# A fused recurrence and long-convolution kernel whose order of work is a table: the table is replaced

## The chip, the core and the metric

The kernel runs on one core of one Trainium2 chip. A core has a matrix engine (TensorE, PE in the profile; its weight loads are shown apart as PEld), a vector engine (VectorE, DVE), a scalar engine (ScalarE, ACT), a general engine (GpSimd, POOL) and SyncE (SP), which here only issues DMA transfers. Matrix results go to PSUM, which has 8 banks; everything else is in SBUF or in device memory. The metric is the device time of one execution in microseconds (us), smaller is better. The kernel before has a median of 460.08 us of three runs, 459.45 to 461.24.

## What is computed

Two layers, one behind the other, on four batches of 6272 steps with 256 channels. The first is a gated linear recurrence, the second a gated long convolution done by Fourier transform:

```python
def _attn_ref(x, f_logit, lower_bound):
    sig = 1.0 / (1.0 + np.exp(-f_logit))
    f = lower_bound + (1.0 - lower_bound) * sig
    for t in range(S):
        h = f[:, t] * h + (1.0 - f[:, t]) * x[:, t]
        y[:, t] = h
def _moe_ref(x, w_proj, filter_fft, w_out):
    x1, x2, x3 = split(x @ w_proj)
    x2_conv = np.fft.irfft(np.fft.rfft(x2, axis=1) * np.fft.rfft(filter_fft, axis=0), axis=1)
    return (x1 * x2_conv * x3) @ w_out
```

## The kernel before

**An order that is data.** The kernel first describes its work as 2410 operations (`op`), each with a kind, the engines that may run it and the tiles it reads and writes. Nothing is scheduled by that: `ORDER` is a string of three-character words, and each word names an operation, an engine and, for TensorE's work, the PSUM bank. `emit` runs through the table and issues the operations one after the other; each engine thus gets its own queue in the order of the table, and works it strictly in that order.

```python
            word = a * 4096 + b * 64 + c
            yield word // 64, self.ENGINES[word // 8 % 8], word % 8
```

**The head.** The filter of 6272 x 256 is loaded in 13 parts (`ff`, L622), rounded where needed (`fr`), rotated by matmuls (`rot`, L637), moved out of PSUM (`f2`), transformed in two steps (`FF1` at L661 with evacuations `afs`, `FF2` at L679 with `hw`), and the spectrum H is stored to device memory (`hst`, L688). Matmuls on a unit matrix (`warm`, L603, two in each operation) compute nothing that is used; the table says where they stand.

**The recurrence** (`hgrn`). Each batch has 13 chunks of 512 steps (the last of 128). A chunk is loaded (`load`, L334: the gate f and then x; three buffers each), goes through the sigmoid on ScalarE (`sig`, L337) and a product on GpSimd (`u`, L339), is turned by transposes on TensorE (`su`, L351, two halves of the channels), the gate is finished (`f`, on ScalarE L364 or VectorE L366), and VectorE scans it (`scan`, L372). The scans of one half of the channels follow each other, chunk by chunk. The beginning of h is copied behind its end (`wrap`, by GpSimd, ScalarE or a DMA issued by SP at L301), since the convolution is cyclic.

**The convolution** of a batch. `P` (L725) applies the part W2 of the projection, 12 groups, and needs all scans of its batch; the evacuations `x2` go to ScalarE (L291) or VectorE (L296). Then 16 units of 8 channel pairs go through a forward transform (`F1`, L737, evacuated by `A`; `F2`, L795), the product with the spectrum loaded from H (`H`, L772; the product directly out of PSUM by VectorE at L816, which the table calls MUL, or a copy and a product `pm` on GpSimd at L825), and the inverse transform (`I2`, L835, evacuated by `Th`). Small operations (`mini`, `zm`, `slot`) treat one special frequency.

**The gates** x1 and x3 (`x13`, L400) run beside it. x1 is always copied out of PSUM (`xs`); x3 is either multiplied with it right out of PSUM by VectorE (MUL, L422), or copied, with the product `z` left to GpSimd (L431).

**The output** (`phase_o`): 13 groups of the last inverse transform (`I1`, L869), the product `y` on VectorE (L875), the output projection (`proj`, L887), its evacuation `o` and the store (L911).

The batches overlap: the chunks of batch b+1 are scanned during the second half of batch b and its output, a stretch that is called a turnover below. A bank is taken again when its evacuation is done, and `SP` issues loads, stores, the reads of H and some of the `wrap` copies in one queue, in the table's order, each waiting there until its tile is free or ready.

## Time and profile before

| | us |
|---|---|
| median of the runs | 460.08 |
| span of the profiled execution | 458.7 |
| TensorE busy | 444.4 |
| VectorE busy | 406.4 |
| ScalarE busy | 400.5 |
| GpSimd busy | 301.9 |

The time of a run is a little above the span, which counts from the first to the last instruction. "Busy" is the time in which at least one instruction of the engine was running. The groups of a profile are given as line, engine, operation, out<-in, shapes and count, then busy time and the mean duration of one in ns, then the idle time of that engine just before them with what ended it. A chain of waits names, from the last instruction back, what each step waited for. Batch 0's `P` begins at 75.5 us, batch 1's at 171, batch 2's at 272.6 and batch 3's at 371.2.

### The profile page before, as it was taken

How to read it: one execution, taken by the hardware profiler on the slowest of the kernel's cores; microseconds unless marked ns; L12 is line 12 of the kernel's file. 1: busy time of each engine (PE TensorE's matmuls, PEld its weight loads, DVE VectorE, ACT ScalarE, POOL GpSimd, SP SyncE). 2: the span in 40 equal slices, each digit the busy share in tenths (PEclk: the TensorE clock that was granted, in tenths of full speed). 3: DMA queues.
4: the chain of work that ended last, by engine and by line, in shares of the span. 5: the costliest groups of instructions: out<-in, count | busy, mean ns of one | idle time of the engine just before them, and what ended most of it. 6: DMA issues, size and time to landing. Idle time of an engine off the chain costs nothing.

```text
span 458.7 us, 14602 instructions
## 1 busy us (share of the span) xinstructions
PE 444.4 (97%) x6009; PEld 346.8 (76%) x6009; DVE 406.4 (89%) x459; ACT 400.5 (87%) x551; POOL 301.9 (66%) x279
## 2 busy tenths in 40 slices
PE   8998999999999999999999999999999999999996
PEld 6777777867766889777668879767768798777785
DVE  8389998699999997999999986999999984999974
ACT  4899998999999988989998969999999869889563
POOL 5377993179899742988996525979896503878500
PEclk9999999999999999999999999999999999999999
DMA  8998999957898898368869897388789542576077
GB/s 321 384 374 300 339 402 372 334 149 210 253 334 273 287 302 325 122 195 298 289 236 317 311 309 298 139 300 282 232 318 307 188 186 93 184 227 201 34 285 292
DMA packets 45298, 121.53 MB, mean 265 GB/s; under 512 B 4400, under 2 KB 8496, under 8 KB 45232
## 3 DMA queue, kind: packets, MB, share of 16 engines
q1 hardware_dynamic: 45232, 120.60, 74.8%
q8 instruction: 47, 0.77, 0.7%
q14 instruction: 19, 0.16, 0.1%
HBM read 86.12 MB, written 31.98 MB: 257 GB/s over the span
## 4 chain that ended last, share of the span: by engine, by line
PE 64%; DVE 12%; ACT 8%; DMA 7%; issue 5%; POOL 2%; SPq 1%; DVEq 0%; ACTq 0%; POOLq 0%
PE PS L400 15%; PE PS L725 9%; PE PS L835 9%; PE PS L351 6%; PE PS L887 6%; PE PS L795 6%; PE PS L737 6%; DVE HA L372 5%; DMA X<-in_moe_filter_fft_dram 4%; DVE ys L875 3%; PE PS L661 3%; DMA XT<-in_x_dram 2%; PE PS L869 2%; ACT fTs L364 2%; DMA out_dram<-PP 2%
## 5 line engine op out<-in xcount | busy, mean ns | idle before, releaser
L339 POOL TENSOR_TENSOR XT<-XT,FL 128x1024 f32<-128x1024 f32 (+1 forms) x49 | 109.7, 2243 | 53.9 <-ACT FL L337 47.3
L372 DVE TENSOR_TENSOR_SCAN HA<-fTs,HA,PS 128x512 f16<-128x512 f32 (+1 forms) x96 | 113.2, 1204 | 1.8 <-ACT fTs L364 1.0
L400 PE MATMUL PS<-HA,W 128*128 128x490 f16 (+1 forms) x416 | 102.9, 368 | 1.7 <-issue 0.7
L825 POOL TENSOR_TENSOR PP<-HA,Hu 98x1008 f16<-98x1008 f16 x40 | 83.9, 2104 | 8.0 <-ACT HA L291 3.9
L291 ACT CAST HA<-PS 128x1024 f16<-128x1024 f32 (+1 forms) x98 | 79.1, 834 | 5.3 <-PE PS L737 2.7
L431 POOL TENSOR_TENSOR zt<-gx 128x490 f16<-128x490 f32 (+1 forms) x37 | 44.9, 1219 | 43.0 <-issue 15.6
L875 DVE TENSOR_TENSOR ys<-PS,zt 128x1024 fp32r<-128x1024 f32 (+1 forms) x52 | 58.7, 1152 | 10.0 <-PE PS L869 7.0
L816 DVE TENSOR_TENSOR PP<-PS,Hu 98x1008 f16<-98x1008 f32 x56 | 65.8, 1202 | 0.9 <-issue 0.5
L364 ACT ACTIVATE fTs<-PS,cc 128x512 f32<-128x512 f32 (+1 forms) x85 | 56.1, 675 | 5.8 <-PE PS L351 4.8
L887 PE MATMUL PS<-Wo,ys 128*128 128x256 f32 x392 | 58.1, 294 | 1.6 <-DVE ys L875 1.3
L400 PEld LDWEIGHTS <-W 128*128 128x128 f16 x416 | 34.8, 97 | 31.6 <-issue 8.1
L835 PEld LDWEIGHTS <-PP 98*128 98x128 f16 x1024 | 50.0, 97 | 10.8 <-issue 1.8
L835 PE MATMUL PS<-VV,PP 98*128 98x98 f16 x1024 | 55.9, 206 | 0.7 <-DVE PP L816 0.5
L887 PEld LDWEIGHTS PS<-Wo,ys 128*128 128x128 f32 x392 | 49.8, 189 | 6.4 <-DVE ys L875 1.4
L291 ACT CAST Th<-PS 128x784 f16<-128x784 f32 x59 | 48.3, 821 | 5.7 <-PE PS L835 5.2
L293 ACT ACTIVATE gx<-PS 128x490 f32<-128x490 f32 (+1 forms) x86 | 49.7, 585 | 2.4 <-PE PS L400 1.0
L337 ACT ACTIVATE FL<-FL 128x1024 f32<-128x1024 f32 (+1 forms) x49 | 49.2, 1009 | 0.0
L422 DVE TENSOR_TENSOR zt<-PS,gx 128x490 f16<-128x490 f32 (+1 forms) x67 | 42.8, 650 | 2.7 <-PE PS L400 1.2
L725 PE MATMUL PS<-W,HA 128*128 128x256 f16 x392 | 44.6, 273 | 0.2
L725 PEld LDWEIGHTS <-HA 128*128 128x128 f16 x392 | 43.0, 142 | 1.2 <-issue 0.2
L351 PE MATMUL PS<-iden,FL 64*128 64x64 f32 x736 | 41.9, 230 | 1.1 <-DVE Hx L296 0.5
L351 PEld LDWEIGHTS PS<-iden,FL 64*128 64x128 f32 x736 | 31.3, 138 | 14.3 <-DVE HA L372 2.6
(129 smaller groups left out, 738.6 us busy)
## 6 DMA issues: line engine op xcount, KB each, us to landing
FL<-in_f_logit_dram SPq DMA_DIRECT2D x45, 512.0 KB, 5.6
XT<-in_x_dram SPq DMA_DIRECT2D x45, 512.0 KB, 6.2
Hu<-H SPq DMA_DIRECT2D x39, 512.0 KB, 4.7
out_dram<-osb SPq DMA_DIRECT2D x22, 512.0 KB, 4.4
out_dram<-PP SPq DMA_DIRECT2D x16, 512.0 KB, 5.2
Hx<-H SPq DMA_DIRECT2D x13, 512.0 KB, 4.5
out_dram<-HA SPq DMA_DIRECT2D x10, 512.0 KB, 4.9
X<-in_moe_filter_fft_dram SPq DMA_DIRECT2D x9, 512.0 KB, 7.3
```

The costliest lines, as they stand in the source:

```text
L291: nc.scalar.copy(dst, src)
L339: op("u", {"POOL": 0.1 + 0.553 * nb}, lambda e, xt=xt, ft=ft: nc.gpsimd.tensor_tensor(xt, xt, ft, op=AOP.mult), r=[("ft", k)], w=[("xt", k)])
L351: nc.tensor.transpose(bank(pb)[:, at[p] + j:at[p] + hn:nb], src[ps, j, cols], iden[ps, ps])
L364: nc.scalar.activation(fT, sT, AF.Identity, scale=by, bias=1.0)
L372: nc.vector.tensor_tensor_scan(h, fT, bank(pb)[:, 512 - hn:512 + hn], init, op0=AOP.mult, op1=AOP.add),
L400: nc.tensor.matmul(PS[:, p, 0:n], W13[:, kh, js], HA[:, HB[kh] + t0:HB[kh] + t0 + n], start=(kh == 0), stop=(kh == 1))
L725: nc.tensor.matmul(pp[:, r - r0, :], column(HB[kh], q_of(r)), W2[:, kh, :], start=(kh == 0), stop=(kh == 1))
L816: nc.vector.tensor_tensor(pr, px.unsqueeze(1).broadcast_to([TB, 2, UE, 63]), hh, op=AOP.mult)
L825: nc.gpsimd.tensor_tensor(pr, spec[:, o, :, 1:64].unsqueeze(1).broadcast_to([TB, 2, UE, 63]), hh, op=AOP.mult)
L835: nc.tensor.matmul(PS[:, ib + o, pr * TB:(pr + 1) * TB], PP[:TB, k, o, n, 2 * pr:2 * pr + 2, :], v[:TB], start=(n == 0), stop=(n == 1))
L875: nc.vector.tensor_tensor(late["ys"][:, yk, :, 0:rn * 128], PS[:, cb:cb + 2, 0:rn * 128], late["zt"][:].rearrange("p k r m -> p k (r m)") ...
L887: nc.tensor.matmul(po[:, i, :], late["ys"][:, yk, kh, i * 128:(i + 1) * 128], Wo[:, kh, :], start=(kh == 0), stop=(kh == 1))
```

## The change

All operations, tiles and functions stay. Only the string `ORDER` is another one. Its first line, before and after:

```diff
 ORDER = (
-    "AAYA+gBFgAMYABIAgVACIBBgAvWBMgAeUBTgAxSAdVBIgAkWBPgA9YANIAmUAoWA/TBGRBADBCYBogBDTBWgAtVAPIBNVAOABagBEDADgBdgBHBBhg"
+    "AAYAlXABIAMYACIANIAhRAPIBTgAkSAiWAaVAfVAgXApQAdVAnSBBgA+gBIgBFgAwXAqSAuUAbSAcXAjXBMgBPgBagBdgBWgA9YBJYBUSAtXArQAeW"
...
 )
```

Decoded, the two tables differ as follows.

| operations | engines before | engines after |
|---|---|---|
| x2 (48) | ScalarE 30, VectorE 18 | ScalarE 24, VectorE 24 |
| xs (208) | ScalarE 117, VectorE 24, direct product 67 | ScalarE 106, VectorE 19, direct product 83 |
| spectrum product (128) | direct 83, copy on VectorE 2, on ScalarE 43 | direct 85, copy on VectorE 0, on ScalarE 43 |
| f2 (13) | ScalarE 11, VectorE 2 | ScalarE 8, VectorE 5 |
| f (104) | ScalarE 85, VectorE 19 | ScalarE 86, VectorE 18 |
| A (64) | ScalarE 55, VectorE 9 | ScalarE 56, VectorE 8 |
| Th (64) | ScalarE 59, VectorE 5 | ScalarE 61, VectorE 3 |
| wrap (48) | GpSimd 26, SP 19, ScalarE 3 | GpSimd 23, SP 25 |

Direct products by batch: 20, 16, 15, 16 before and 21, 22, 16, 24 after. 1285 operations keep their engine and get another PSUM bank. On TensorE 559 of the 770 operations stand in another place, by three places on average; on VectorE the operations that both tables give it move by at most four places. TensorE changes between kinds that use half of its rows (transposes, F2, I1, FF2) and kinds that use all of them 252 times before and 250 times after. The larger moves on the queues, in the order in which each engine works (* is a count):

```text
TensorE, head, before:  warm*8 rot*3 warm rot*3 warm*3 rot warm*2 rot*5 warm*2 rot warm*3 FF1*4 warm FF2 FF1 warm FF2 FF1 su ...
TensorE, head, after:   warm*16 rot warm*4 rot warm rot warm rot*3 warm rot*2 warm*2 rot*5 warm FF1*4 FF2 FF1*3 FF2 su*2 ...
TensorE, batch 0, before:  x13*7 P*12 x13*4 F1*2 ...   (around last)
TensorE, batch 0, after:   x13*5 P*5 x13 P x13 P x13 P*2 x13 P*3 x13*3 F1*2 ...
TensorE, tail, before:  I1 proj*2 warm*5 I1 proj
TensorE, tail, after:   I1 proj I1 proj*2 warm*4
SP, filter and first loads, before:  ff0 2 1 4 6 3 5 12 7 8, lower_bound, ff9 10 11, then loads
SP, filter and first loads, after:   ff6 1 0 3 2 4 5 8 9 7 10 11, lower_bound, ff12, then loads
SP, end of batch 2, before:  f11 x11 store f/x12 ...   (x12 ahead of f12)
SP, end of batch 2, after:   f11 store f12 x11 x12 store ...
```

The last two lines name the loads of the last two chunks of batch 3, f for the gate and x for the input.

More of the change, by code (lines that the diff above doesn't have):

```diff
@@ L193 @@
+    "kgRkdskYokhPkipkjYidNigYikYilSkkUkPYdFQklXkUYkZYkmMknvkoYimCkpSkeYkqKdGAk4UkuQkzWkvIkrSksCk0OkwQk9Sk1Wk5Mk6Uk2GkxI"
+    "k+KlCQlHWk/Sk7ElDIlEUlMQlACdHgktglFEk3gkygk8glBglGglIOlNIlRSlJWlKGlSKlOUlPElLglQglWQlXIlbSlTWlYUlgQlUGlcKlVglZElag"
+    "lhIldSllUliQleClfglmMlnSloKlpgA8XA5XA4XA6XljAlkg"
 )
```

123 lines of the change are left out of this document (60 added, 63 removed).

## The prediction

> **What bounds the kernel now.** I read first the page's busy line and the line on the chain that ended last, then one table of stretches with each engine's busy time, cut where the chain changes character.
>
> ```profile
> span 458.7 us, 14602 instructions
> PE 444.4 (97%) x6009; PEld 346.8 (76%) x6009; DVE 406.4 (89%) x459; ACT 400.5 (87%) x551; POOL 301.9 (66%) x279
> PE 64%; DVE 12%; ACT 8%; DMA 7%; issue 5%; POOL 2%; SPq 1%; DVEq 0%; ACTq 0%; POOLq 0%
> ```
> TensorE is idle for 458.7 - 444.4 = 14.3 us of the span and carries 64% of the chain. The profiled execution spans 458.7 us; the median of the runs is 460.08, so 1.4 us lies around the span, and I add it at the end.
>
> ```profile
> core 0: us, PE busy (x) PEld busy (x) DVE busy (x) ACT busy (x) POOL busy (x), PEclk, DMA share, GB/s
> 0.00:23.35 23.35, 20.99 (x111) 16.51 (x112) 13.73 (x44) 16.21 (x17) 10.78 (x29) 1.00 0.92 353
> 23.35:35.60 12.25, 12.15 (x132) 9.56 (x134) 10.42 (x12) 11.14 (x14) 9.59 (x12) 1.00 0.97 357
> 35.60:56.00 20.40, 18.62 (x266) 14.57 (x266) 19.67 (x22) 19.93 (x30) 17.08 (x14) 1.00 0.91 321
> 56.00:75.50 19.50, 19.45 (x228) 14.38 (x229) 19.20 (x23) 18.89 (x28) 15.93 (x23) 1.00 1.03 382
> 75.50:86.20 10.70, 10.70 (x100) 10.65 (x99) 5.73 (x6) 9.09 (x11) 0.00 (x0) 1.00 0.96 344
> 86.20:130.00 43.80, 43.09 (x637) 30.90 (x634) 41.56 (x46) 41.30 (x60) 34.35 (x30) 1.00 0.75 236
> 130.00:171.00 41.00, 39.18 (x639) 30.05 (x633) 40.40 (x42) 38.37 (x57) 31.82 (x24) 1.00 0.87 294
> 171.00:243.00 72.00, 71.89 (x966) 54.39 (x966) 67.09 (x71) 65.85 (x96) 56.98 (x46) 1.00 0.71 249
> 243.00:272.60 29.60, 28.49 (x488) 24.27 (x489) 28.92 (x29) 24.80 (x34) 15.32 (x11) 1.00 0.91 301
> 272.60:343.00 70.40, 70.00 (x948) 52.61 (x949) 64.36 (x70) 66.67 (x96) 57.21 (x47) 1.00 0.76 270
> 343.00:371.20 28.20, 26.83 (x474) 23.09 (x471) 27.11 (x27) 24.19 (x33) 14.30 (x9) 1.00 0.70 244
> 371.20:381.60 10.40, 10.40 (x96) 10.09 (x96) 5.69 (x5) 7.09 (x9) 0.00 (x0) 1.00 0.36 141
> 381.60:431.80 50.20, 50.18 (x645) 36.07 (x646) 45.11 (x55) 43.61 (x63) 38.52 (x37) 1.00 0.47 151
> 431.80:458.70 26.90, 22.45 (x314) 19.66 (x312) 17.40 (x17) 13.33 (x14) 0.00 (x0) 1.00 0.65 260
> ```
> Three kinds of stretch stand here. In the middle of each batch (171 to 243, 272.6 to 343, 381.6 to 431.8) TensorE is busy to within 0.4 us: it is the bound, and its work is the same in both tables. In the turnovers from one batch to the next (243 to 272.6, 343 to 371.2, the end of 130 to 171) VectorE is busy to within 1.1 us, with the scans of the next batch and the products y of this one, and TensorE loses 1.11, 1.37 and at most 1.82 us. The third is the head and the tail, where TensorE loses 2.36 us up to 23.35, 1.78 from 35.6 to 56, and 4.45 after 431.8. So nothing that only reorders can give more than about 14 us less what must start and drain; the reachable part is the idle time of 86.2 to 371.2 (0.71 + 1.82 + 0.11 + 1.11 + 0.40 + 1.37 = 5.5) and some 4 of the head.
>
> **The change, part by part.** The two tables hold the same 2410 operations. They differ in three ways.
>
> *Engines.* Read off the tables: VectorE gets 6 more evacuations x2 (ScalarE 6 fewer), 16 more direct products x1*x3 (the MUL form), each of which takes a copy x3 away (11 fewer on ScalarE, 5 on VectorE) and a product z on GpSimd; three f2 move from ScalarE to VectorE; two spectrum products become direct. The prices:
>
> ```profile
> L431 POOL TENSOR_TENSOR zt<-gx 128x490 f16<-128x490 f32 (+1 forms) x37 | 44.9, 1219 | 43.0 <-issue 15.6
> L816 DVE TENSOR_TENSOR PP<-PS,Hu 98x1008 f16<-98x1008 f32 x56 | 65.8, 1202 | 0.9 <-issue 0.5
> L293 ACT ACTIVATE gx<-PS 128x490 f32<-128x490 f32 (+1 forms) x86 | 49.7, 585 | 2.4 <-PE PS L400 1.0
> L422 DVE TENSOR_TENSOR zt<-PS,gx 128x490 f16<-128x490 f32 (+1 forms) x67 | 42.8, 650 | 2.7 <-PE PS L400 1.2
> L291 ACT CAST X<-PS 128x1024 f16<-128x1024 f32 (+1 forms) x30 | 31.5, 1092 | 9.4 <-PE PS L725 7.0 <-DVE ys L875 2.4
> L296 DVE CAST X<-PS 128x1024 f16<-128x1024 f32 x18 | 21.6, 1222 | 11.8 <-PE PS L725 11.8
> ```
> VectorE: 6 x 1.22 + 16 x 0.65 - 5 x 0.65 + 3 x 1.22 + 2 x 1.2, less a few small ones that go the other way, about +14 us. ScalarE about -13 (6 x 1.09 + 11 x 0.585). GpSimd -16 x 1.22 = -19.5 and more. On the end this costs nothing as long as TensorE covers it: four of the six x2 and the three extra products beside them fall into the stretches where W2 is applied (75.5 to 86.2 and 371.2 to 381.6), where VectorE works 5.7 of 10.5 us. Eight of the 16 direct products are in the last batch. There, from 381.6 to 431.8, VectorE gets 6 x 0.65 + 2 x 1.2 and loses 4 x 0.65 and a copy of some 0.7, so 45.1 becomes about 48.1 of 50.2 us. That still fits, narrowly; what it costs if not is a rival below. Value taken: 0.
>
> *The head.* The table before has 8 pairs of warming matmuls (L603) ahead of the first rotation of the filter (L637), and 7 pairs between the transforms FF1 and FF2 after 23.35. The new table has 16 ahead of the first rotation, 9 among the rotations, one behind them and none after FF1 has begun; 26 in both.
>
> ```profile
> 1.34 3.60 PE L603 MATMUL PS<-iden 128*128 128x256 f16 x16 [1.34 <-POOL iden masks.py:199]
> 4.86 4.03 PE L637 MATMUL PS<-X,rot 128*128 128x256 f32 x16
> 22.09 0.36 PE L637 MATMUL PS<-afs,rot 128*128 128x256 f32 x1
> 22.29 0.83 PE L603 MATMUL PS<-iden 128*128 128x256 f16 x6
> 23.35 2.14 PE L661 MATMUL PS<-D1r,f 128*128 128x256 f32 x16 [0.23 <-DVE f L296]
> ```
> The first 16 matmuls took 4.86 - 1.34 = 3.5 us, 0.22 each; six later ones took 0.83 with their latency, about 0.12 each. Eight more pairs ahead of the first rotation thus cost between 16 x 0.12 = 1.9 and 16 x 0.22 = 3.5 us; I take 2.1, near the lower end, since the rotations themselves run at the later pace. The Trainium skill (TensorE: Matmul & The Clock Gate, Part 1) says that the array's clock is halved until about 3.4 us of activity; by it three of the added sixteen would be slow and the rest fast, 2.2 us. The trace agrees on the two paces; no run here shows the point in between.
>
> From 4.86 to 22.29 TensorE had the rotations and 8 pairs of warming matmuls among them (about 1.9 us), so 15.5 us of rotations, some 0.9 of it waiting. In the new table: 4.86 + 2.1 + 14.6 + 9 x 0.23 = 23.6 for their end against 22.29, so FF1 begins up to 1.3 us later. If the rotations wait less than I think, it is 0.3; I take +0.9.
>
> After that the 7 pairs are gone:
>
> ```profile
> L603 PE MATMUL PS<-iden 128*128 128x256 f16 x6 | 1.2, 278 | 0.0
> L603 PE MATMUL PS<-iden 128*128 128x256 f16 x8 | 1.4, 272 | 0.5 <-ACT Hx L291 0.5
> ```
> The first row is 23.35 to 35.6, where TensorE is busy 12.15 of 12.25 us: 3 x 0.23 = -0.7. The second is 35.6 to 56, where VectorE (19.67 of 20.4) and ScalarE (19.93) set the pace: 4 pairs, between 0 and -0.9, taken at -0.45. Head: 0.9 - 0.7 - 0.45 = -0.25.
>
> *The order in the batches.* Before, the twelve matmul groups of W2 in batch 0 (75.5 to 86.2) run in a row; now four groups of x1/x3 stand between them (two of them stood ahead before), whose evacuations use VectorE's free 5 us there, and two are gone from 86.2 to 130, where TensorE idles 0.71. Between 0 and -0.7, taken at -0.7 as VectorE is full there (41.56 of 43.8). In the turnovers of batches 0 and 1 one gate f of 128 columns leaves VectorE for ScalarE each:
>
> ```profile
> L366 DVE TENSOR_SCALAR fTs<-PS,cc 128x128 f32<-128x128 f32 x1 | 0.3, 350 | 0.0
> ```
> 2 x 0.35 = -0.7, since VectorE is the bound there and ScalarE has 4.8 us free (24.80 of 29.6). Everything else is a shift by two or three places on each engine, and the new PSUM banks follow it; I have no row that gives it a sign: between -2 and +3 us, taken at 0.
>
> *The tail.* Five warming pairs (5 x 0.23 = 1.1 us) that stood ahead of the last I1 are gone from there (four now follow the last projection), and the last y no longer stands behind an evacuation on VectorE. But the end is a store:
>
> ```profile
> 452.68 2.06 SPq L911 DMA_DIRECT2D out_dram<-osb  x2
> 455.90 0.33 SPq L911 DMA_DIRECT2D out_dram<-PP  x1
> ```
> In the new order the last store is a full group's of 512 KB, not the small one of 128 KB, issued about 454.6. The store that began in the table before in the pair of 452.68 landed some 3 us later, so it would end where it ends now. Between -1.1 and +0.5; taken at 0.
>
> Sum: -0.25 - 0.7 - 0.7 = -1.65, so a span of 457.0 and a median of 458.4; I say **458.2**.
>
> **The rivals.** (1) *A load that comes too late, slower.* At the end of batch 2 the new SP queue issues the f part of chunk 12 ahead of the x part of chunk 11. The former's buffer comes free one chunk later.
>
> ```profile
> 353.03 9.28 DMA XT<-in_x_dram
> ```
> ```profile
> 356.40 0.33 SPq L334 DMA_DIRECT2D XT<-in_x_dram  x1
> 356.82 0.76 SPq L334 DMA_DIRECT2D FL<-in_f_logit_dram  x1
> ```
> ```profile
> XT<-in_x_dram SPq DMA_DIRECT2D x45, 512.0 KB, 6.2
> ```
> The x load of chunk 11 was issued at 353.03 and was on the chain for 9.28 us, until GpSimd's product of that chunk could start. Behind chunk 12 it is issued no earlier than 356.4, 3.4 us later. If it takes the median 6.2 us, it lands at 362.6, 0.3 late; if 9.3 again, 3.4 us late, and all of it counts, for the scans of the last chunks wait. It decides from a landing time of 5.9 us on. For it: the chain runs through just this load. Against it: the stores that shared the engines with it are now issued behind the loads. Time: 460.1 + 3.4 = 463.5.
>
> (2) *VectorE becomes the bound in the last batch, slower.* It needs 48.1 us of the 50.2; where it is busiest beside a full TensorE it reached 93% (67.09 of 72). At 93% the stretch takes 51.7, +1.5; at the 90% it has there now, 53.4, +3.2. Time 461.6 to 463.3. The Trainium skill (Perfetto Trace Analysis, Identifying the Most-Contended Engine) speaks for it: busy time of matmuls is no measure of TensorE's room, that of the weight loads is, and that is 76% here, below VectorE's 89%. The chain speaks against it: in the stretches at 100% TensorE it runs through matmul after matmul.
>
> (3) *The head loses what it must not, slower.* If the 16 added matmuls all run at 0.22 (3.5 us), the rotations end at 25.0, 2.7 later than now; if the pairs taken out behind them lay in time that VectorE and ScalarE set anyway, nothing comes back: 460.1 + 2.7 = 462.8.
>
> (4) *The search found more.* If half of the 5.5 us of reachable idle time and 2 us of the head go, -5: 455. For it: nearly every stretch is within 1 us of a full TensorE or VectorE, so each wait removed counts. Against it: the waits are many and short, and the same number of evacuations has to be made in the same time.
>
> (5) *It does nothing that shows*: 460.
>
> **How the numbers follow.** About 0.5% (2.3 us, 457.8 to 462.4) is what a measurement can tell from no change. The forecast has 0.45: its own range is 455.5 to 462.5, of which 0.20 is faster by more, 0.23 within and 0.02 slower. Rival 4: 0.20, all faster. Rival 5: 0.04, within. Rival 1: 0.17 and rival 3: 0.06, slower; rival 2: 0.08, the upper half of its times slower. Faster 0.20 + 0.20 = 0.40; same 0.23 + 0.04 + 0.04 = 0.31; slower 0.02 + 0.17 + 0.06 + 0.04 = 0.29. The range from 453 to 464.5 takes in rivals 1 and 4 with the bounds of the unknown shifts, and leaves about a fifth out.
>
> **What would show it.** Right: FF1's first matmul between 23.6 and 24.7; no L603 between 25 and 75; VectorE above 95% in the last batch's middle while TensorE stays at 100%; the turnovers 0.3 us shorter each; GpSimd some 25 us less busy with no change of the span. Wrong: the span of a middle stretch longer by more than a microsecond with TensorE idle in it; a load of x on the chain with more than 10 us at the end of batch 2; FF1 before 23.

## The result, and the profile after

| | before | after |
|---|---|---|
| median of four runs, us | 459.76 | 470.85 |
| lowest and highest | 459.37 to 461.24 | 469.84 to 475.01 |
| span of the profiled execution | 458.7 | 468.1 |

The changed kernel is slower: after to before 1.0254, 95% interval 1.0207 to 1.0302. The runs of the old kernel lie within 1.9 us, those of the new one within 5.2; the slowest of these has a mean granted clock of 0.983, the three others 0.991 or 0.992. First the page of the kernel after: span, busy line, chain.

```profile
span 468.1 us, 14557 instructions
PE 446.0 (95%) x6009; PEld 349.4 (75%) x6009; DVE 419.8 (90%) x473; ACT 388.2 (83%) x534; POOL 277.9 (59%) x258
PE 46%; DVE 8%; DMA 5%; ACT 4%; issue 3%; POOL 1%; SPq 0%; DVEq 0%; ACTq 0%; POOLq 0%
```

The engines moved as forecast: VectorE has 13.4 us more, ScalarE 12.3 and GpSimd 24.0 less. TensorE has the same work and is idle for 22.1 us in place of 14.3. To see where, both kernels are cut at the first matmul of P (L725) in each batch. The stretches of the kernel before (columns as in the prediction's table of stretches):

```profile
0.00:75.36 75.36, 71.06 (x731) 54.88 (x732) 62.88 (x99) 66.04 (x86) 53.38 (x77) 1.00 0.95 353
75.36:170.97 95.61, 93.08 (x1365) 71.70 (x1364) 87.80 (x93) 88.88 (x126) 66.17 (x53) 1.00 0.82 273
170.97:271.51 100.54, 99.35 (x1443) 77.83 (x1441) 94.95 (x98) 90.68 (x129) 72.30 (x56) 1.00 0.77 265
271.51:371.21 99.70, 97.90 (x1424) 76.56 (x1424) 92.57 (x97) 90.88 (x128) 71.51 (x56) 1.00 0.74 262
371.21:458.67 87.46, 83.02 (x1051) 65.81 (x1050) 68.19 (x76) 64.03 (x85) 38.52 (x37) 1.00 0.52 184
```

and of the kernel after:

```profile
0.00:77.80 77.80, 70.87 (x727) 55.91 (x728) 64.66 (x99) 63.22 (x84) 53.89 (x77) 0.98 0.93 351
77.80:175.12 97.32, 94.10 (x1369) 73.03 (x1368) 91.30 (x94) 86.15 (x124) 63.99 (x50) 1.00 0.78 270
175.12:275.72 100.60, 98.93 (x1443) 77.33 (x1441) 94.42 (x99) 90.27 (x128) 65.74 (x51) 1.00 0.78 270
275.72:379.10 103.38, 99.25 (x1431) 78.06 (x1429) 93.62 (x98) 90.14 (x127) 69.36 (x53) 0.98 0.71 256
379.10:468.06 88.96, 82.86 (x1046) 65.11 (x1045) 75.78 (x86) 58.38 (x74) 24.92 (x27) 1.00 0.48 169
```

The second column is the length: head +2.44, batch 0 +1.71, batch 1 +0.06, batch 2 (with the turnover to batch 3) +3.68, batch 3 +1.50, together 9.4. In two of the five the granted clock is no longer 1.00. Finer stretches of the kernel after, in the head and at the end of batch 2:

```profile
28.00:32.00 4.00, 3.87 (x53) 3.03 (x51) 3.50 (x4) 3.63 (x6) 3.91 (x5) 1.00 0.30 93
...
48.02:51.43 3.41, 1.29 (x30) 1.16 (x26) 1.80 (x2) 2.07 (x4) 1.62 (x6) 1.00 1.03 414
51.43:54.84 3.41, 3.41 (x28) 2.19 (x27) 2.69 (x3) 2.62 (x6) 2.83 (x3) 0.50 1.04 409
...
368.87:372.28 3.41, 1.83 (x37) 1.63 (x35) 2.13 (x2) 1.92 (x4) 2.99 (x2) 1.00 0.35 137
372.28:375.70 3.42, 3.42 (x43) 3.08 (x42) 1.87 (x2) 1.54 (x4) 0.00 (x0) 0.50 0.27 108
```

From 28 to 32 us the DMA engines move 93 GB/s; the kernel before moved 345 there:

```profile
28.00:32.00 4.00, 4.00 (x58) 3.34 (x60) 3.71 (x4) 2.92 (x6) 4.00 (x6) 1.00 0.95 345
```

From 48 to 51.4 the DMA engines are saturated and every engine starves, TensorE with 1.29 of 3.41 us. Then the granted clock is half for 3.41 us. The same follows at 372.28. A stretch of 3.41 us at half clock, if TensorE sets the end there, costs about 1.7 us (half of it, an estimate) on top of what starved it.

Why were the DMA engines empty at 28 us? SP's queue in the kernel after:

```profile
30.50 0.33 SPq L334 DMA_DIRECT2D FL<-in_f_logit_dram  x1
30.88 0.43 SPq L473 DMA_DIRECT2D HA<-in_moe_w_proj_dram  x1
34.06 0.33 SPq L334 DMA_DIRECT2D FL<-in_f_logit_dram  x1
34.44 0.91 SPq L334 DMA_DIRECT2D XT<-in_x_dram  x2
```

The first row is the gate of chunk 4, which waits until 30.50 for its buffer. The weights w_proj (768 KB) wait for nothing but stand behind it; so does the x of chunk 4, which moreover stands behind the gate of chunk 5. In the kernel before w_proj was issued at 18.92:

```profile
18.92 0.38 SPq L473 DMA_DIRECT2D HA<-in_moe_w_proj_dram  x1
```

At the end of batch 2 it is the x of chunk 11, behind the gate of chunk 12. The chain of waits of the kernel after, some of its links in order of time:

```profile
361.73 0.33 SPq L334
...
362.11 6.55 DMA XT<-in_x_dram
...
368.82 2.36 POOL XT L339
371.22 0.46 PE PS L351 x8
```

The gate goes out at 361.73 and the x right behind it; GpSimd's product and the transposes wait for it. Measured from the batch's first P it is issued at 362.11 - 275.72 = 86.4 us, before at 353.03 - 271.51 = 81.5.

So three suspects: SP's queue, the half clock that follows, and VectorE in the last batch, beside the four engines' own order. A fourth, the store that comes last, shows itself below.

### The profile page after: what moved, and what is told of

It reads as the page before. It is cut to its first block, busy times and chain, and to the rows that moved or that the text cites. A ratio compares the mean times of both kernels' runs of the same rounds, so it can differ in the third digit from the quotient of the medians.

```text
span 468.1 us, 14557 instructions
## 1 busy us (share of the span) xinstructions
PE 446.0 (95%) x6009; PEld 349.4 (75%) x6009; DVE 419.8 (90%) x473; ACT 388.2 (83%) x534; POOL 277.9 (59%) x258
## 4 chain that ended last, share of the span: by engine, by line
PE 46%; DVE 8%; DMA 5%; ACT 4%; issue 3%; POOL 1%; SPq 0%; DVEq 0%; ACTq 0%; POOLq 0%
PE PS L400 10%; PE PS L887 7%; PE PS L835 7%; PE PS L725 5%; PE PS L737 5%; PE PS L795 4%; PE PS L351 4%; DMA FL<-in_f_logit_dram 4%; DVE HA L372 3%; PE PS L869 3%; DVE zt L422 2%; DMA XT<-in_x_dram 1%; DVE ys L875 1%; ACT fTs L364 1%; ACT FL L337 1%
## 5 line engine op out<-in xcount | busy, mean ns | idle before, releaser
L339 POOL TENSOR_TENSOR XT<-XT,FL 128x1024 f32<-128x1024 f32 (+1 forms) x49 | 109.7, 2241 | 80.2 <-ACT FL L337 49.7
L400 PE MATMUL PS<-HA,W 128*128 128x490 f16 (+1 forms) x416 | 108.5, 368 | 1.0 <-ACT Th L291 0.7
L291 ACT CAST HA<-PS 128x1024 f16<-128x1024 f32 (+1 forms) x99 | 80.2, 836 | 5.6 <-PE PS L795 2.6
L825 POOL TENSOR_TENSOR PP<-HA,Hu 98x1008 f16<-98x1008 f16 x38 | 79.8, 2104 | 6.3 <-ACT HA L291 2.9
L816 DVE TENSOR_TENSOR PP<-PS,Hu 98x1008 f16<-98x1008 f32 x58 | 67.8, 1198 | 0.5 <-POOL zt L431 0.2
L835 PEld LDWEIGHTS <-PP 98*128 98x128 f16 x1024 | 50.8, 97 | 13.2 <-issue 3.2
L422 DVE TENSOR_TENSOR zt<-PS,gx 128x490 f16<-128x490 f32 (+1 forms) x83 | 52.9, 649 | 5.2 <-PE PS L400 3.3
L835 PE MATMUL PS<-VV,PP 98*128 98x98 f16 x1024 | 56.4, 206 | 0.4 <-DVE PP L816 0.2
L291 ACT CAST Th<-PS 128x784 f16<-128x784 f32 x61 | 49.9, 820 | 6.9 <-PE PS L835 5.6
L400 PEld LDWEIGHTS <-W 128*128 128x128 f16 x416 | 32.8, 97 | 23.1 <-issue 5.9
L351 PE MATMUL PS<-iden,FL 64*128 64x64 f32 x736 | 43.0, 232 | 3.6 <-ACT Hx L291 1.1
L351 PEld LDWEIGHTS PS<-iden,FL 64*128 64x128 f32 x736 | 32.5, 140 | 17.5 <-issue 3.4
L725 PE MATMUL PS<-W,HA 128*128 128x256 f16 x392 | 44.9, 273 | 0.4 <-ACT X L291 0.2
L725 PEld LDWEIGHTS <-HA 128*128 128x128 f16 x392 | 43.1, 142 | 2.0 <-issue 0.6
L800 POOL TENSOR_TENSOR PP<-zp 98x32 f16<-98x32 f16 x64 | 19.3, 337 | 37.6 <-DVE zp L761 31.1
```

What stands on the lines that cost most here:

```text
L291: nc.scalar.copy(dst, src)
L339: op("u", {"POOL": 0.1 + 0.553 * nb}, lambda e, xt=xt, ft=ft: nc.gpsimd.tensor_tensor(xt, xt, ft, op=AOP.mult), r=[("ft", k)], w=[("xt", k)])
L351: nc.tensor.transpose(bank(pb)[:, at[p] + j:at[p] + hn:nb], src[ps, j, cols], iden[ps, ps])
L400: nc.tensor.matmul(PS[:, p, 0:n], W13[:, kh, js], HA[:, HB[kh] + t0:HB[kh] + t0 + n], start=(kh == 0), stop=(kh == 1))
L422: nc.vector.tensor_tensor(zd(), px, xs(0), op=AOP.mult)
L725: nc.tensor.matmul(pp[:, r - r0, :], column(HB[kh], q_of(r)), W2[:, kh, :], start=(kh == 0), stop=(kh == 1))
```

## The experiments

In what follows f and x are the loads of gate and input of a chunk in SP's queue. Every kernel was profiled once and timed beside the kernel before; the table gives the median, its ratio to the kernel before, and from the profile the first P of batch 0, the lengths of the four batches (P to P, the last to the end of the span) and where the clock fell to half ahead of the tail.

| kernel | us | ratio, 95% | P of batch 0 | batches 0, 1, 2, 3 | clock falls at |
|---|---|---|---|---|---|
| before | 459.8 | | 75.36 | 95.61 100.54 99.70 87.46 | - |
| after | 470.9 | 1.0254 [1.0207, 1.0302] | 77.80 | 97.32 100.60 103.38 88.96 | 51, 372 |
| e1 | 464.2 | 1.0102 [1.0064, 1.0140] | 80.48 | 95.83 100.56 98.89 87.29 | 47 |
| e2 | 470.7 | 1.0244 [1.0222, 1.0267] | 76.34 | 97.48 105.14 101.48 89.59 | 50, 258 |
| e3 | 470.4 | 1.0228 [1.0193, 1.0262] | 76.12 | 97.19 103.04 102.39 89.54 | 47 |
| e4 | 470.7 | 1.0230 [1.0168, 1.0292] | 78.96 | 96.74 101.66 101.11 89.29 | 48 |
| e5 | 464.8 | 1.0108 [1.0083, 1.0133] | 80.46 | 95.60 101.36 99.78 87.44 | 7 |
| e6 | 470.4 | 1.0242 [1.0211, 1.0273] | 85.71 | 95.61 100.38 98.77 87.10 | 10 |
| e7 | 471.6 | 1.0261 [1.0240, 1.0283] | 74.89 | 101.45 101.10 103.70 88.88 | 91, 375 |
| e8 | 463.4 | 1.0083 [1.0067, 1.0099] | 76.00 | 95.61 100.10 100.12 89.24 | - |
| e9 | 477.6 | 1.0381 [1.0362, 1.0400] | 74.53 | 106.07 102.40 102.42 89.44 | 91, 173 |
| e10 | 461.8 | 1.0039 [1.0022, 1.0055] | 75.53 | 95.82 100.25 98.78 89.64 | - |
| e11 | 468.2 | 1.0189 [1.0148, 1.0231] | 75.33 | 97.00 103.00 101.26 89.44 | - |
| e12 | 475.8 | 1.0354 [1.0333, 1.0375] | 74.97 | 103.83 102.17 101.84 89.25 | 92 |
| e13 | 468.3 | 1.0198 [1.0157, 1.0240] | 74.89 | 97.03 101.63 103.92 88.88 | 370 |
| e14 | 459.7 | 1.0008 [0.9993, 1.0023] | 75.26 | 95.58 100.55 98.79 87.57 | - |
| e15 | 473.7 | 1.0293 [1.0247, 1.0338] | 74.67 | 97.77 102.82 102.43 92.97 | - |
| e16 | 460.5 | 1.0024 [1.0011, 1.0037] | 75.71 | 96.79 100.15 100.45 87.23 | - |
| e17 | 463.6 | 1.0094 [1.0063, 1.0125] | 75.06 | 96.65 99.80 100.44 88.93 | - |
| e18 | 458.8 | 0.9985 [0.9970, 0.9999] | 75.07 | 95.60 100.11 98.78 87.37 | - |

### The head

**e1: the new head alone.**

```diff
-the new table throughout
+the new table up to the first P of batch 0, then the old one
```

> The new table up to the first P group of batch 0, the old one from there on. In the new kernel that P began 2.44 us later than before (77.80 against 75.36). If the head's loss is one of its own and the batches carry it unchanged, this kernel takes 459.8 + 2.4 = 462.2 us, and its last batch has full clock. If the head also leaves buffers and loads in a worse state, so that batch 0's 1.7 us belong to it, 463.9. If batch 0 makes up for a late start, 460 to 461. The clock's fall at 51.4 must be there in the first two cases.

Measured 464.2 us, runs from 462.0 to 466.2. The batches have the old lengths again: the head's loss is its own, and batch 0's is not. The profiled run had two falls in a row (6.83 us), and its P begins 5.1 us late.

**e2: w_proj first.**

```diff
-SP: f4 w_proj f5 x4 x5
+SP: w_proj f4 x4 f5 x5
```

> The new table with two entries of SP's queue moved: the load of w_proj (768 KB) ahead of the gate load of chunk 4, behind which it waited until 30.9 us, and the x load of chunk 4 ahead of the gate load of chunk 5. Late loads as the cause: the DMA engines work from 20 to 31, the load of f for chunk 6 lands earlier, the stretch 47.4 to 50.8 has TensorE busy for more than 2.3 of 3.4 us (1.43 now), the clock stays full at 51.4, and P of batch 0 begins 1.5 to 2.5 us earlier: 468.3 to 469.4 us. The missing warming pairs as the cause: the clock falls all the same, and the time stays at 470.9 within 0.7.

Half of each: P began at 76.34, 1.5 earlier than in the kernel after (one head begins P up to 5 us apart from profile to profile, see e13), but the clock fell all the same (at 49.6) and once more in batch 1, and the time stayed. The hole only moved, to 36 to 40 us (DMA share 0.61).

**e3: warming pairs back.**

```diff
-TensorE: warm*16 rot ... FF1*4 FF2 FF1*3 FF2 su*2 ...
+TensorE: warm*9 rot ... FF1*4 warm FF2 FF1 warm FF1*2 FF2 su*2 ...
```

> The new table with seven of the warming pairs that it has ahead of the first rotation put back between FF1 and the start of P, each behind the operation that it stood behind in the old table; no load is moved. The missing pairs as the cause of the clock's fall: the clock stays full between 50 and 56 and the batch's P begins 1.7 us earlier, 469.2 us. Late loads as the cause: the fall at 51.4 stays (within 1.5 us of that place), the rotations begin 1.6 to 2 us earlier but P of batch 0 begins at 77.0 to 77.8, and the time is 470 to 470.9.

Some of the pairs moved here write into banks that hold a result of FF1 or of the transposes, so part of the spectrum and of the gates is overwritten. The clock fell at 47.0, which is 4.4 us ahead of 51.4 and not within 1.5 of it; FF1 begins 2.0 us earlier, P 1.7. The pairs do not hold the clock.

**e14: the pairs out of the old head**, the cleaner form of the same question.

```diff
-TensorE: warm*8 rot*3 ... FF1*4 warm FF2 FF1 warm FF2 FF1 su ...
+TensorE: warm*15 rot*3 ... FF1*4 FF2 FF1 FF2 FF1 su ...
```

> The old table with one change: the seven warming pairs between FF1 and the first P of batch 0 stand ahead of the first rotation, as in the new one. If these pairs keep the clock up there, it falls between 30 and 60 us and the time is 461.5 to 463.5 us. If they are only 1.6 us of work, the clock stays full; FF1 begins 1.2 to 1.6 later and P of batch 0 within 0.7 us of 75.4: 459 to 460.5 us.

Measured 459.7, ratio 1.0008. The stretch from FF1 to P in e14, without a warming pair, has the full clock:

```profile
23.70:75.26 51.56, 48.44 (x606) 37.33 (x607) 49.04 (x55) 49.92 (x70) 42.70 (x48) 1.00 0.96 354
```

**e5 and e6: queue against engines.** e5 is the old table with the new order of SP's queue in the head; e6 the new head with the old order of it, and the old table from P on.

```diff
-SP in e5: ff0 2 1 4 ..., f0 f1 x0 f2 x1 x2 w_proj f3 x3 f4 x4 f5 x5 ...
+SP in e5: ff6 1 0 3 ..., f2 f0 x0 f1 f3 x1 x2 x3 f4 w_proj f5 x4 x5 ...
-SP in e6: ff6 1 0 3 ..., the loads as in the line above
+SP in e6: ff0 2 1 4 ..., the loads as in the first line
```

> The old table; only the order of SP's queue up to the first P of batch 0 is the new one (loads, stores of H, wrap copies); every other engine keeps its old order, its warming pairs and its banks. The queue's order as the cause of the head's loss: P of batch 0 begins 2 to 5 us later than at 75.36, with the DMA engines below 0.5 somewhere between 28 and 40 and at 1.0 behind it, the clock falls between 43 and 52, and the time is 462 to 465 us (464.2 with the whole new head). The warming pairs and the engines as the cause: the clock stays full, P begins within 0.7 us of 75.4, 459.4 to 460.1 us.

> The counterpart: the new head on TensorE, VectorE, ScalarE and GpSimd (warming pairs and engines of f2 among it), but SP's queue up to the first P in the old order, and the old table from that P on. The queue as the cause: the clock stays full up to the end and the time is 459.0 to 460.5 us. The warming pairs and the engines as the cause: the clock falls between 43 and 55 as in the whole new head, 462 to 466 us. Half and half (either alone starves the engines): about 462.

e5 took 464.8, as much as the whole new head (464.2), with every engine in its old order: the stretch from FF1 to P took 54.84 us in place of 52.01, at a full clock, with the DMA share at 0.21 and 0.54 in the two stretches of 4 us from 28 and 32. So the queue costs 2.8 us there without any fall. The rest of e5's delay is none of the new kernel's: its filter too is loaded in the new order, which the old rotations do not follow, the clock falls once at 7.4, and FF1 begins at 25.62, 2.3 us later than before. That e5 and e1 come out alike is therefore in part chance. e6 has the same fault the other way round: its old queue loads the filter in an order that the new rotations do not follow, so FF1 begins at 32.07, and its 470.4 says nothing of the engines.

**e9: old loads under the new head.** Only the transfers behind the filter's keep the old order.

```diff
-SP: ff6 1 0 3 ... f2 f0 x0 f1 f3 x1 x2 x3 f4 w_proj f5 x4 x5 ...
+SP: ff6 1 0 3 ... f0 f1 x0 f2 x1 x2 w_proj f3 x3 f4 x4 f5 x5 ...
```

> The whole new table, but in SP's queue up to the first P of batch 0 everything behind the filter's thirteen loads stands in the old order (w_proj ahead of the gate load of chunk 3, each chunk's x directly behind its gate, stores of H later). The filter's own loads keep the new order, which the new rotations need. The queue as what the new head loses: no hole in the DMA engines between 28 and 40, the clock stays full through 43 to 56, and P of batch 0 begins at 75.5 to 76.5 in place of 77.8 to 79; the time is 3 to 4 us less than the new kernel's 470.9: 467 to 468. The warming pairs and engines as the cause: P still begins behind 77.5, and the time stays within 0.7 of 470.9.

The head did what the queue's theory says: P at 74.53, no fall. And yet 477.6. Batch 0 took 106.07, for the reason in one row of ScalarE's timeline in e9:

```profile
89.86 1.06 ACT L337 ACTIVATE FL<-FL 128x1024 f32<-128x1024 f32 x1 [4.88 <-DMA FL<-in_f_logit_dram]
```

The new order has ScalarE take a sigmoid of batch 1 among the evacuations of P; the old queue loads that gate later. ScalarE waits 4.88 us, the evacuations of P stand behind it, TensorE waits for them, and the clock falls for 6.83 us. **e7**, the old head with the new rest, stumbled at the same place.

```diff
-the old table throughout
+the old table up to the first P of batch 0, then the new one
```

> The old table up to the first P of batch 0, the new one from there on. The new head with the old rest took 464.2, 4.8 us more than the old kernel. If the head's loss and that of the batches add, this one takes 470.9 - 4.8 = 466.1 us, with the loss in batches 1 to 3 as in the profiles of the new tables: 2 to 4 us at each of the two last turnovers and 1.5 to 2 in the last batch. If the batches lose only because the head leaves them late, 460 to 462.

At the seam two evacuations of x1 and x3 read another bank than their matmuls wrote. Its 471.6 contain a wait of 3.5 us for the same gate, which neither table alone has; the other batches are as long as the new table's. The order of a queue is right or wrong only for the engines that consume it.

### The last batch

**e8: the new last batch alone.**

```diff
-the old table throughout
+the old table up to the first P of batch 3, then the new one
```

> The old table up to the first P of batch 3, the new one from there on, with the last batch's eight more direct products on VectorE. VectorE as the bound of that batch: it is busy above 96% between 381 and 432, the batch takes 1.5 to 2 us longer than the old 87.5, 461.0 to 461.5 us. The batch only slow because it starts with late data: at most 0.4 us longer, 459.4 to 459.8.

At the seam one y of batch 2 reads another bank than its matmuls wrote. Batch 3 took 89.24, 1.8 more, at a full clock; the whole 3.6 more (463.4, above the expected 461.5), of which the profile shows another 0.6 ahead of P and leaves the rest open. VectorE was busy for 95% of the middle stretch, 47.61 of 50.20 us.

**e10: the products alone.**

```diff
 batch 3, eight x3:
-copied out of PSUM by ScalarE or VectorE, multiplied by GpSimd
+multiplied straight out of PSUM by VectorE, in their old places
```

> The old table with one change: eight more x3 of batch 3 are multiplied straight out of PSUM by VectorE (24 in place of 16, as in the new table), in their old places. VectorE as the bound of the last batch: its P-to-end time goes from 87.5 to 88.5 to 89.5 us, VectorE above 96% from 381 to 432, 461 to 462 us. The order in the last batch as the cause: 459.4 to 460.0, or less.

461.8, and batch 3 took 89.64, 2.2 more than before. By its size this is the last batch's loss; by its place it is not. In the stretch that begins 10.4 us behind P, which in the kernel before is the row 381.60:431.80 of the prediction, the kernel after and e10 have

```profile
389.50:439.70 50.20, 49.71 (x641) 34.93 (x640) 47.61 (x60) 41.03 (x57) 24.92 (x27) 1.00 0.44 138
```

```profile
380.78:430.98 50.20, 49.51 (x625) 34.98 (x626) 45.88 (x57) 41.40 (x58) 29.05 (x29) 1.00 0.45 151
```

In both, TensorE still shows 49.7 and 49.5 of 50.2 us busy, and the busy time of its weight loads (the next number) fell alike, from 36.07 to 34.93 and 34.98. But the counts differ: 645 matmuls before, 641 in the kernel after, 625 in e10. So does the end of the last inverse transform (the last matmul of L835): 60.65 us behind P before, 62.85 in e10, but 60.72 in the kernel after and 60.69 in e8. In the old places the eight products thus hold TensorE up by 2.2 us, with VectorE at 45.88 of 50.20 us (91%, not the expected 96%); which wait does it was not followed. In the new places, with VectorE at 47.61, they hold up nothing.

What the new table loses in batch 3 comes at the very end. The last projections of the kernel before and of the kernel after, from their chains of waits:

```profile
454.90 0.52 PE PS L887 x2
```

```profile
460.86 1.45 PE PS L887 x10
```

They end 84.2 us behind P before and 83.2 after: TensorE is done 1.0 us sooner. Then the last two stores of the kernel after, from SP's queue, and the two stretches from the issue of the last store to the end of the span, before and after:

```profile
462.86 0.33 SPq L911 DMA_DIRECT2D out_dram<-PP  x1
463.28 0.41 SPq L911 DMA_DIRECT2D out_dram<-osb  x1
```

```profile
455.90:458.67 2.77, 0.00 (x0) 0.00 (x0) 0.00 (x0) 0.00 (x0) 0.00 (x0) 1.00 0.36 138
```

```profile
463.28:468.06 4.78, 0.00 (x0) 0.00 (x0) 0.00 (x0) 0.00 (x0) 0.00 (x0) 0.98 0.51 199
```

The store issued last is the small one of 128 KB before, a full one of 512 KB after. It is issued 0.5 us sooner behind P (84.2 in place of 84.7) but lands 3.8 us later in place of 1.7, and the span ends 1.5 us later. So it is in every profile. In the eleven with the new last batch (all of the new table but e15, and e8) the last projection ends at 83.2 to 83.5, the last store lands 3.6 to 4.3 us after its issue, and the span ends at 88.9 to 89.6; in the seven with the old last batch (without e10) these are 83.8 to 84.2, 1.7 to 1.9 and 87.1 to 87.6. No run exchanged the two stores alone.

**e15: the products back, in the new places**, with the queue mended as in e13 below.

```diff
 batch 3 of the kernel with the mended queue:
-24 direct products of VectorE
+16 (two products of GpSimd moved ahead of the copy that reuses their buffer)
```

> The kernel with the 22 moved entries, and in batch 3 the x3 products on VectorE back to the sixteen of the old table (the eight others copied out and multiplied on GpSimd). Costs that add: 1.7 to 2.2 us less than that kernel, the last batch at 87.3 to 87.9. If GpSimd's products come too late in the new places: the last batch at 88.5 to 90, no gain.

The last batch took 92.97, 4.1 more than with the direct products. GpSimd waits once for 17.7 us behind VectorE's y there, but it does so for 15.0 in the kernel before too; the last inverse transform ends 65.68 us behind P, 5.0 later than in e13, and what holds it up was not followed further. The new places do not suit the old engines: what was searched together cannot be mixed at will.

### The turnovers

**e4: the x of chunk 11 first.**

```diff
-SP, end of batch 2: f11 store f12 x11 x12 store
+SP, end of batch 2: f11 x11 store f12 x12 store
```

> The new table with one entry of SP's queue moved: the x load of chunk 11 of batch 3 directly behind the gate load of chunk 11, ahead of a store and of the gate load of chunk 12, as in the old table. Late load as the cause of the end of batch 2 and of the clock's fall at 372.3: it is issued at about 358.9 in place of 362.1, TensorE's wait of 1.57 us for GpSimd's product is gone, the clock stays full in batch 3, batch 3's P begins 2 to 3 us earlier and takes 1.7 us less: 466.2 to 467.2 us. VectorE with the scans and y as the bound of that turnover: at most 0.7 us is gained, and the clock falls somewhere else there: 470.2 to 470.9.

No fall there and batch 2 at 101.11, but the time is 470.7, runs from 466.4 to 471.9: inconclusive. Kernels that keep the late x without a fall there (e2, e3, e9) have 101.5 to 102.4, so this load is worth about a microsecond.

**e11 and e12: the old order of loads** in the turnovers (e11), and there and in the head (e12).

```diff
-SP, batch 3: x0 f0 f2 f1 x2 x1 x3 x4 f3 f5 x5 f4 x6 f6 f8 x7 f7 x8 ... f11 f12 x11 x12
+SP, batch 3: f0 x1 f1 f2 x0 x2 x3 f3 f4 x4 f5 x5 f6 x6 x7 f7 f8 x8 ... f11 x11 x12 f12
```

> The whole new table, but the loads of batches 1, 2 and 3 behind the first P of batch 0 stand in the old order among the places that loads have in SP's queue; stores, copies and reads of H keep theirs. Late loads as the cause of the turnovers' loss: no fall of the clock between 250 and 275 or between 340 and 380, batch 2 (P to P) takes 99.7 to 100.7 us in place of 101 to 103.4, and the time is 2 to 4 us less than 470.9: 467 to 469. VectorE or the stores as the cause: within 0.7 of 470.9.

> The changes of the two kernels on loads together: the new table's engines, places and banks on the four working engines, but the old order of the loads in the head and in the turnovers. If late loads make all of the loss but the last batch's: head 76, batches 0 to 2 within a microsecond each of 95.6, 100.5 and 99.7, the last 89.3: 462 to 463.5 us, no fall of the clock before the end, and runs within 1 us of each other (the old kernel's are; the new one's lie 5 us apart). If places and engines lose by themselves in the turnovers: 465 to 468.

e11: 468.2, as expected for late loads, with no fall of the clock ahead of the tail, but batch 2 stayed above the expected 100.7, at 101.26, batch 1 took 103.00, and the intervals of e11 and of the kernel after overlap. Its span of 466.0 is still 7.3 above the kernel before. So the half clock is not the larger part. e12 stumbled as e9 did (batch 0 at 103.83).

**e13: no ready load behind one that waits.**

```diff
-SP, batch 0: f2 f0 x0 f1 f3 x1 x2 x3 f4 w_proj f5 x4 x5 f6 x6 f7 f8 x7 ...
+SP, batch 0: f2 f0 x0 f1 f3 x1 x2 x3 w_proj f4 x4 f5 x5 f6 x6 f7 x7 f8 ...
-SP, batch 3: x0 f0 f2 f1 x2 x1 x3 x4 f3 f5 x5 f4 ... f11 f12 x11 x12
+SP, batch 3: x0 f0 f1 x1 f2 x2 x3 f3 x4 f4 f5 x5 ... f11 x11 f12 x12
```

> The new table with 22 of SP's 267 entries moved: every load whose buffer is free earlier in the table than that of an entry ahead of it goes ahead of that entry (w_proj ahead of the gate load of chunk 4, x ahead of the next gates, in batch 3 the gate load of chunk 4 eight places up, the x load of chunk 11 one). No engine, no bank and no other order changes. If what the new table loses outside its last batch is loads that stand ready behind an entry that is not, this kernel has P of batch 0 at 75 to 76, batches 0 to 2 within 1 us each of 95.6, 100.5 and 99.7, the last batch at 89.4: 461.8 to 464 us, and runs within 2 us of each other. If the four engines' own order loses by itself (the kernel with the turnover loads exchanged had a full clock throughout and still took 1.4, 2.5 and 1.6 us more in batches 0 to 2): 466 to 469.

The head no longer loses: P at 74.89, in e15 and e17, which have the same queue, 74.67 and 75.06. With the new head unchanged it was 75.33, 77.80, 78.96 and 80.48 in four profiles (e11, after, e4, e1), with no, one, two and two steps of 3.41 us at half clock. From 28 us e13 has

```profile
28.00:32.00 4.00, 3.56 (x62) 2.72 (x62) 3.67 (x4) 3.63 (x7) 3.93 (x5) 1.00 0.97 346
```

As in e2 a smaller hole stays at 36 to 40 us (DMA share 0.66), but no fall follows it. Batches 1 and 2 took 101.63 and 103.92, and the total is 468.3. GpSimd in e13 waits again for an x, now that of chunk 10:

```profile
360.63 2.38 POOL L339 TENSOR_TENSOR XT<-XT,FL 128x1024 f32<-128x1024 f32 x1 [4.36 <-DMA XT<-in_x_dram]
```

The load stands behind no other load, only behind two copies and a store whose issue takes 1.9 us, but it is late all the same: issued 80.7 us behind P, in the kernel before 76.8. The second half of batch 2, cut 56 and 80 us behind P, in the kernel before, in the kernel after and in e13:

```profile
327.51:351.51 24.00, 23.85 (x382) 17.88 (x378) 23.55 (x28) 22.29 (x36) 19.59 (x15) 1.00 0.87 299
351.51:371.21 19.70, 18.37 (x314) 15.68 (x315) 18.74 (x20) 16.29 (x22) 9.54 (x7) 1.00 0.66 232
```

```profile
331.72:355.72 24.00, 22.91 (x363) 16.69 (x361) 22.66 (x26) 21.37 (x34) 20.28 (x15) 1.00 0.67 239
355.72:379.10 23.38, 20.98 (x337) 18.40 (x337) 19.99 (x20) 17.84 (x24) 7.82 (x4) 0.93 0.79 294
```

```profile
329.55:353.55 24.00, 23.12 (x367) 16.71 (x364) 22.86 (x26) 21.61 (x34) 20.71 (x15) 1.00 0.68 236
353.55:377.47 23.92, 21.32 (x340) 18.79 (x339) 20.14 (x21) 18.14 (x24) 7.85 (x4) 0.93 0.77 287
```

The last column: in 24 us the old order moves 299 GB/s, the new ones 239 and 236, which is 24 x 60 = 1.4 MB less. What is missing is mostly stores. The old queue issues three in these 24 us, 57.2, 57.7 and 75.6 us behind P; in the kernel after the first two (of batch 1) went out by 17.5, and the third (the first of batch 2) goes out at their very end, at 79.8. Of the loads it is that of x10 that leaves the stretch, issued at 80.5. Two reads of H come into it. The last stretch then has to move more: 23.38 x 294 = 6.9 MB in the kernel after, 19.70 x 232 = 4.6 MB before. The new order also scans chunk 6 later (from 75.2 us behind P, before from 73.0).

**e17 and e18: a quarter of the stores**, in e13 and in the old table.

```diff
-out[b][:, r0:r0+rn, :] = o[:, 0:rn, :]   in batches 0 to 2
+out[b][:, r0:r0+1, :] = o[:, 0:1, :]
```

> The new table with SP's queue mended (22 entries), and the stores of batches 0 to 2 write only the first of their four rows, a quarter of the bytes; the rest of those batches' output is left out. Every order stays. If the new turnovers lose because their loads come late in the stretch and meet the stores there (DMA engines at 1.0 from 353 to 365 in the kernel with the full stores, GpSimd waiting 4.4 us for one x load): loads of x at the end of batch 2 take 3 to 5 us in place of 6 to 9, batches 1 and 2 take 99.5 to 101 us each (101.6 and 103.9 with the full stores), no fall of the clock, 463 to 465 us. If the order of the four engines loses by itself: batches 1 and 2 within 0.7 us of those values but for the clock, 467 to 469.

> The old table with the same cut of the stores of batches 0 to 2, for comparison: it moves its loads earlier in each batch, so the stores should cost it less. If that is so: 0.3 to 1.5 us less than the old kernel, 458 to 459. If the stores cost both tables the same: as much less as the new table gains, 3 to 5 us: 454.5 to 456.5.

e17: 463.6, 4.7 less than e13; batches 1 and 2 at 99.80 and 100.44. e18: 458.8, 0.85 less than the kernel before beside it. With the same orders on the four engines, 4.7 us come back to the new table and 0.85 to the old. The x of chunks 10, 11 and 12 land 5.2, 6.1 and 4.0 us after their issue (3 to 5 were expected), in e13 6.2, 8.4 and 7.3. In the kernel before they take as long as in e13 (6.7, 9.3 and 7.3), but are issued 3.9, 3.5 and 1.9 us sooner behind P. The second half of batch 2 in e17:

```profile
327.51:351.51 24.00, 22.85 (x363) 16.39 (x361) 22.59 (x26) 21.33 (x34) 20.59 (x15) 1.00 0.67 238
351.51:371.95 20.44, 19.99 (x341) 17.34 (x340) 20.21 (x21) 18.09 (x24) 7.91 (x4) 1.00 0.58 188
```

The first half of it is as thin as in e13 (238 GB/s); with fewer stores the second takes 20.44 in place of 23.92, of which the step at half clock that e13 has there (at 370.2) can be up to 1.7. So what the last part of these turnovers lost is mostly the meeting of late loads with the stores and the fall of the clock that follows. That evacuations wait for a store to free their buffer is a smaller part: 1.0 us in that stretch of e13.

**e16: the same rule on the old queue.**

```diff
-SP, batch 1, among transfers of H: f0 ... pre f1 ... x1 ... x0 ...
+SP, batch 1: x0 f1 x1 and ten more loads ahead of an entry that is not ready
```

> The old table with the same rule applied to SP's queue (13 loads move ahead of an entry that is not ready). If the old table too loses through loads that stand behind others, 1 to 2 us less: 458 to 459. If its loads are early enough: within 0.5 us of the old kernel. If the earlier loads take the DMA engines from those that are needed first, up to 1.5 us more.

460.5, ratio 1.0024: 1.1 us slower, batch 0 at 96.79. The old table's loads were early enough; sooner is not better where the DMA engines are full. No kernel of these was faster than the kernel before, but for e18, which leaves out stores.

## Why the prediction was wrong

The forecast was 458.2 and the range 453 to 464.5; the kernel takes 470.9, 11.1 more than the kernel before. Going by the runs, some 4 us of that are late loads that meet the stores, 1.6 the store that comes last, some 2.6 SP's queue (not clear of the scatter), and the rest is open. Step by step:

- **The term for all other shifts failed**: "Everything else is a shift by two or three places on each engine, and the new PSUM banks follow it; I have no row that gives it a sign: between -2 and +3 us, taken at 0." In it lay SP's queue and the time at which loads and stores go out. Going by medians, mending the queue takes 470.9 to 468.3 and the cut stores take that to 463.6, less the 0.85 that they also give the old table: 2.6 and 3.9 us. The first of the two is smaller than the scatter of these kernels (the intervals of after and e13 overlap); what speaks for it is the head, 74.7 to 75.1 in three profiles with the mended queue against 75.3 to 80.5 in four without. The row for the sign stood in the prediction: its table of stretches has DMA shares of 0.91 to 1.03 up to 86.2 us, so there is little room to make good what is not moved. In the two stretches of 4 us from 28 us e5 leaves them idle for 5.0 us and loses 2.8 at a full clock; in e11, whose head is that of the kernel after, the share from 28 to 32 is 0.50, the clock stays full and nothing is lost.
- **The tail, taken at 0, failed**: "so it would end where it ends now", between -1.1 and +0.5. The prediction saw that a full store would be last, put its issue 1.3 us ahead of the small one's and its landing some 3 us behind that. The issue came 0.5 us sooner, the landing 3.8 behind it, and the end 1.5 later: the whole loss of batch 3.
- **"On the end this costs nothing as long as TensorE covers it"** held in batch 3 of the new table: VectorE's 48.1 of 50.2 us came out as 47.6, and TensorE was done 1.0 us sooner. Rival 2, at 0.08 and with +1.5 to +3.2, did not come true there; that batch 3 lost 1.5 us, the size that it named, is chance. It came true in e10, where the same products stand in the old places (+2.2). The sentence that spoke for it fits e10: the Trainium skill (Perfetto Trace Analysis, Identifying the Most-Contended Engine) does not take the busy share of matmuls for a measure of TensorE's room, and e10 lost 2.2 us with matmuls 99% busy. The weight loads, which it names in place of them, tell e10 from the kernel after by their number (626 and 640), not by the busy time in the profile (34.98 and 34.93 us).
- **"it is the bound, and its work is the same in both tables"**, said of TensorE in the middle of each batch, held in batch 3 alone. From P to the end of the last inverse transform the kernel after takes 71.96, 69.08, 70.61 and 60.72 us in batches 0 to 3, the kernel before 69.91, 68.20, 68.99 and 60.65. Part of that is work moved across this border (932 matmuls become 937 in batch 1). But in batch 2 TensorE is idle for 1.42 us of it in place of 0.43, and a longer middle with TensorE idle was named as a sign of being wrong.
- **Head, -0.25**: the eight added pairs took 2.76 us in place of 2.1 (the rotations begin at 7.62, before at 4.86), since the granted clock rose only at 7.06, before at 5.55: some ten of the sixteen matmuls went at the slow pace, not three. FF1 was put 0.9 later and came 1.13 later (24.48), inside the stated 23.6 to 24.7. The seven pairs behind it, -1.15, were worth about half where the queue does not interfere: from FF1 to P e13 took 51.44 and e14 51.56 against 52.01, -0.6 and -0.45. The queue and the clock's fall turned this into +1.31.
- **P with x13 between, -0.7**: batch 0 is 1.4 longer in e13 and 1.0 in e17 against e18. **Turnovers, -0.7**: from the last inverse transform to the next P batches 0 and 1 are 0.3 and 0.8 us shorter in the kernel after, as forecast, but the stretches ahead of that are longer by more (2.1 and 0.9).
- **Rival 1** named the right load and mechanism at the end of batch 2 but one instance of it, +3.4 us. That x was issued 4.9 us later in its batch, yet e4 shows it worth about 1: other loads were late too (x10 by 3.7 us).
- **Rival 3**, the head losing 2.7 us, met the size (+2.44) for another reason: FF1 came 1.13 later, and the rest stands behind it. The losses came together; the range let each come alone.
- **Not considered**: the fall of the clock. It follows the starvation and adds to it, but is not the cause: the profile of e11 has no fall ahead of the tail and a span 7.3 us longer, and e5 loses 2.8 us between FF1 and P at a full clock.

**Open**: of the 463.6 - 458.8 = 4.8 us between e17 and e18, the two profiles show 1.6 in batch 3 (the last store), 1.7 in batch 2 and 1.0 in batch 0, and 0.3 gained in batch 1. In batches 0 and 2 the loss stands there by the end of the last inverse transform (1.6 and 2.0 us), ahead of the last part of the turnover. No run tells whether engines, places or banks cause it.

## What to carry to other kernels

Where transfers share one in-order queue, ask of each what stands ahead of it and when that becomes ready, and do so against the engines' order that consumes it: the old queue under the new engines was worse (477.6) than either table. Where the DMA engines show above 0.9, an order is also a schedule of bytes: loads that go out later meet the stores, and no engine's busy share shows it. A busy TensorE is not proof that it is the bound, and a loss of the expected size is not proof of its cause: count the matmuls of a stretch, and compare when a given piece of work ends in both kernels. At the end of a kernel, what is stored last counts in full.

## What the runs showed of the hardware

The granted clock changes in steps of 3.41 us, counted from where it first rises, in all 20 profiles: the three stretches at full clock in the kernel after, 44.37, 317.44 and 92.16 us, are 13, 93 and 27 such steps. Every step at full clock in which TensorE was busy less than 0.48 was followed by a step at half clock; of those between 0.48 and 0.62 some were and some not (0.614 in e3 was, 0.482 in e2 was not); above 0.62 none was. The lowest of the kernel before, between head and tail, was 0.79, so it never fell. The Trainium skill (TensorE: Matmul & The Clock Gate, Part 1) describes the return to half rate as following an idle window of about 3.4 us; the window's length agrees, but here a half-busy one was enough (0.54 at 368.87).

In the tail, with no engine at work, the last store of 512 KB landed 3.8 us after its issue in the kernel after, the last one of 128 KB 1.7 us after its issue in the kernel before.
